# Feed-forward rows kept in PSUM, exponentials added before the row sum, a 128x9 reciprocal, and zero matmuls in PE's early gaps

## The chip, the core and the metric

The kernel runs on one core of one Trainium2 chip. The metric is device time in microseconds (us), from several timed runs, beside one execution that the hardware profiler recorded. PE is TensorE (matmuls), PEld its weight loads, DVE is VectorE, ACT is ScalarE, POOL is GpSimd, and SP issues the DMAs. PSUM is the accumulator memory that PE writes and that DVE and ACT read; SBUF is the working memory.

## The reference

Causal attention with a decaying bias over 8 batches of 8 heads (576 positions, head size 64), then a gated feed-forward on the joined heads:

```
cum    = cumsum(max(s, 0))
scores = q k^T / 8 + min(cum_k - cum_q, 0), causal
attn   = exp(scores - rowmax) / (sum + 1e-9)
x      = heads joined (attn v)                  # 576 x 512 per batch
h      = relu(x @ w_in)                         # 576 x 1024
conv   = sum over k of conv_w[k] * h shifted by k - 1 rows
out    = (h * sigmoid(conv)) @ w_out
```

## The kernel before

The 64 heads are worked as 32 pairs, four pairs to a batch. A pair p goes through these steps. Scores for the row maxima are made on PE into pairs of PSUM banks (`sh{p}.{i}`, lines 1089 to 1102) and reduced on DVE (lines 1124 and 1134); the maxima are transposed and come back by DMA as a shift row (`eq<-rt`, line 1179). Scores for the output are made transposed, keys on partitions (`sc{p}.{i}`, line 1211), and ACT turns them into exponentials in the tile `pt` (line 1233), in five blocks of keys t = 0 to 4 with 576, 448, 320, 192 and 64 query columns. The row sums (`sum{p}`, line 1289) are matmuls of `pt` with a one-hot matrix of 32 columns; the four quarters of the 576 queries, 144 columns each, go to four strips of the array, and the two heads run through the strips in opposite order. The product with v follows (`pv{p}`, line 1271). ACT copies the sums with a guard added (`gd{p}`, line 1308), DVE takes the reciprocal of the 128x144 tile (`inv{p}`, line 1313; only eight of its rows mean anything), SP stores it to DRAM (line 1318) and spreads it back to all partitions (line 1327, two DMAs), and DVE multiplies (`nm{p}`, line 1335). The high and low parts of the result become the tile `x` (lines 1350 and 1354).

The feed-forward works on halves of a batch. For each of eight blocks of 128 hidden columns a tile of 12 matmuls fills one PSUM bank (`h{b}.{hf}.{f}`, line 1386). ACT writes relu of it into the SBUF tile `ht` (line 1397), which frees the bank. Everything behind that is from SBUF: the scaled copy (line 1409), two taps on DVE (line 1422), one sigmoid for two blocks (line 1438), the product with `ht` (line 1444), and the split into high and low parts of `u` (lines 1451 and 1455). Output matmuls read `u` (`o{b}.{hf}.{m}.{fp}`, line 1483, 24 for a bank) and ACT or DVE evacuates them (line 1500).

Six PSUM banks (`ps`) serve all of this but `pv`, which has two of its own. The order on each engine isn't that of the program: `Sched.play` runs a list scheduler over all steps with assumed durations and the dates in the table `DUE`, and instructions are issued on each engine in the order that it finds; the semaphores then make each wait for its inputs. A bank is given to a step when the plan says that its last user is done. From pair 8 on, PE runs a pair's steps as one burst in a fixed order, which nothing else may interrupt:

```
ORDER = ("sh0", "sum", "pv", "sh1", "sc0", "sh2", "sc1", "sc2", "sh3", "sc3")
```

where `sum` and `pv` are of the pair before. The plan marks DVE and POOL steps that may disturb each other and doesn't let them overlap. It also models a slower PE after a rest (`REST`, `WARM`). `stay_awake` can fill PE's planned gaps until the time `AWAKE`; with `AWAKE = 0.0` it does nothing. In the first 160 us or so the weights are loaded as 64-bit words and taken apart on DVE, ACT and POOL (lines 863 to 952) beside the attention of the first pairs.

## Time and profile before

| | us |
|---|---|
| median of 3 runs (805.84 to 806.18) | 806.12 |
| the profiled execution | 809.6 |
| its span, first to last instruction | 807.9 |
| PE busy | 774.9 |
| DVE busy | 544.8 |
| ACT busy | 439.5 |
| POOL busy | 328.7 |

The profiled execution is 3.5 us longer than the median, and 1.7 us longer than its span. Busy times are modelled from the records; matmuls overlap, so a busy PE need not be PE at its peak.

### The profile page before, as it was taken

To read this page: it belongs to the slowest core of one execution; us is meant where nothing else is said; L and a number is where in the kernel's file an instruction comes from. 1 tells how busy PE (TensorE), PEld (TensorE's weight loads), DVE (VectorE), ACT (ScalarE), POOL (GpSimd) and SP (SyncE) were. 2 spreads that over 40 slices of the span, in tenths; PEclk is the share of its full clock that TensorE was granted. 3 is DMA by queue.
4 is the path that set the end of the run, shared out by engine and by line. 5 is a ranking of instruction groups with operands and counts; after the bars stand their busy time and mean duration, and the time that the engine had idled before them with its cause. 6 is when DMAs were issued, how large, how long until landed. Compare 5 with 4: busy or idle time off the path is not lost.

```text
span 807.9 us, 21422 instructions
## 1 busy us (share of the span) xinstructions
PE 774.9 (96%) x8557; PEld 690.7 (85%) x8557; DVE 544.8 (67%) x1310; ACT 439.5 (54%) x989; POOL 328.7 (41%) x508
## 2 busy tenths in 40 slices
PE   2899899999999999999999999999999999999998
PEld 1566566898999989998998989998898989998998
DVE  7789979747675867766566757667576576825532
ACT  5355446746455646546555646646554555744543
POOL 7122324344534455544435445553435454422122
PEclk9999989999999999999999999999999999999999
DMA  7654354221423232241414233241414221111001
GB/s 241 209 146 150 109 153 145 86 83 46 141 68 124 77 119 96 79 138 53 141 49 132 87 111 105 75 137 57 140 49 125 96 84 43 43 35 42 17 29 37
DMA packets 57369, 78.77 MB, mean 97 GB/s; under 512 B 6521, under 2 KB 39609, under 8 KB 57209
## 3 DMA queue, kind: packets, MB, share of 16 engines
q1 hardware_dynamic: 57269, 77.40, 30.2%
q8 instruction: 67, 1.10, 0.6%
q14 instruction: 33, 0.27, 0.1%
HBM read 63.94 MB, written 13.19 MB: 95 GB/s over the span
## 4 chain that ended last, share of the span: by engine, by line
PE 90%; DVE 4%; ACT 3%; DMA 1%; issue 1%; POOL 0%; SPq 0%; ACTq 0%; DVEq 0%; POOLq 0%
PE ps L1483 26%; PE ps L1386 25%; PE ps L1211 15%; PE pv L1271 11%; PE ps L1289 7%; PE ps L1089 4%; DVE ps L1134 2%; DMA ek<-bx 1%; PE ps L1101 1%; PE ps L1215 1%; ACT pt L1233 1%; PE ps L1095 1%; PE ps L1160 0%; ACT bx L784 0%; DVE ct L880 0%
## 5 line engine op out<-in xcount | busy, mean ns | idle before, releaser
L1483 PE MATMUL ps<-u,wo 128*128 128x288 f32 x1536 | 220.3, 299 | 0.7 <-ACT ob L1500 0.5
L1386 PE MATMUL ps<-x,wi 128*128 128x290 f32 x1536 | 217.5, 298 | 0.3 <-ACT pt L1233 0.2
L1422 DVE SCALAR_TENSOR_TENSOR ct<-ht,cw_sb,ct 128x288 f32<-128x288 f32 (+1 forms) x256 | 154.6, 617 | 84.7 <-ACT ct L1409 81.2
L1483 PEld LDWEIGHTS ps<-u,wo 128*128 128x128 f32 x1536 | 208.3, 188 | 3.6 <-ACT ob L1500 0.7
L1386 PEld LDWEIGHTS ps<-x,wi 128*128 128x128 f32 x1536 | 209.7, 190 | 1.4 <-ACT pt L1233 0.6
L1233 ACT ACTIVATE pt<-ps,bias_sb 128x288 f32<-128x288 f32 (+4 forms) x384 | 154.3, 478 | 88.7 <-PE ps L1211 88.1
L1455 POOL TENSOR_TENSOR u<-ct,u 128x576 fp32r<-128x576 f32 x64 | 94.2, 1477 | 234.2 <-ACT u L1451 201.0
L1134 DVE CUSTOM_DVE_ANT_0 ps<-ps,bb 128x288 f32<-128x288 f32 (+2 forms) x260 | 108.3, 454 | 60.0 <-PE ps L1089 30.6
L1211 PE MATMUL ps<-s 64*128 64x288 f32 (+4 forms) x1152 | 122.8, 309 | 5.7 <-DVE r L1134 4.2
L1066 POOL TENSOR_SCALAR_AFFINE_SELECT bb<-bb 128x256 f32<-128x256 f32 (+1 forms) x130 | 59.4, 466 | 129.5 <-DVE r L1134 102.3
L1211 PEld LDWEIGHTS ps<-s 64*128 64x128 f32 x1152 | 98.3, 190 | 15.7 <-DVE r L1134 10.0
L1025 POOL TENSOR_TENSOR s<-raw,s 128x1152 fp32r<-128x1152 f32 x31 | 83.2, 2684 | 48.1 <-DVE s L1021 36.8
L1271 PE MATMUL pv<-pt,v 128*32 128x448 f32 (+4 forms) x1536 | 96.6, 395 | 1.0 <-DVE rb L1335 1.0
L1397 ACT ACTIVATE ht<-ps 128x289 f32<-128x289 f32 x128 | 52.7, 411 | 80.0 <-PE ps L1386 79.3
L1271 PEld LDWEIGHTS pv<-pt,v 128*32 128x32 f32 x1536 | 60.0, 111 | 33.0 <-issue 26.2
L1246 POOL TENSOR_SCALAR_AFFINE_SELECT pt<-pt 128x128 f32<-128x128 f32 (+1 forms) x240 | 67.7, 302 | 22.0 <-ACT pt L1233 20.4
L1211 PE MATMUL ps<-eq,ek 64*128 64x288 f32 (+4 forms) x384 | 68.5, 323 | 0.0
L1409 ACT ACTIVATE ct<-ht,cw_sb 128x288 f32<-128x288 f32 x121 | 64.9, 536 | 5.4
L1089 PE MATMUL ps<-s 64*128 64x288 f32 (+4 forms) x384 | 61.9, 345 | 3.7 <-DVE r L1134 1.8
L1289 PE MATMUL ps<-pt,onehot 128*32 128x144 f32 (+4 forms) x1792 | 61.4, 273 | 0.2 <-ACT pt L1233 0.2
L1438 ACT ACTIVATE ct<-ct 128x576 f32<-128x576 f32 x64 | 43.5, 680 | 31.4 <-DVE ct L1422 30.6
L1289 PEld LDWEIGHTS ps<-pt,onehot 128*32 128x32 f32 x1792 | 54.8, 113 | 6.5 <-issue 1.1
(90 smaller groups left out, 671.0 us busy)
## 6 DMA issues: line engine op xcount, KB each, us to landing
raw<-qk SPq DMA_DIRECT2D x32, 576.0 KB
bb<-cum_d SPq DMA_DIRECT2D x26, 576.0 KB
v<-vp SPq DMA_DIRECT2D x32, 320.0 KB
rb<-ri_d SPq DMA_DIRECT2D x64, 144.0 KB
outT<-ob SPq DMA_DIRECT2D x64, 144.0 KB
ht<-w_out SPq DMA_DIRECT2D x16, 256.0 KB
w<-w_in SPq DMA_DIRECT2D x8, 512.0 KB
ri_d<-ri SPq DMA_DIRECT2D x32, 72.0 KB
```

The source lines that it names most:

```text
L1025: tt_on(e)(st[:, 0:2, :], R_t[raw.slot], st[:, 2:4, :].bitcast(F32), op=ALU.subtract)
L1089: nc.tensor.matmul(dst[j], l, S_t[sb.slot][r, 2, c0:c1], start=True, stop=not early)
L1134: nc.vector.tensor_tensor_reduce(out=src, in0=src, in1=in1, scale=1.0, scalar=acc if c0 else -3.0e38, op0=ALU.add, op1=ALU.max, accum_out=acc,
L1211: nc.tensor.matmul(dst[j], l, m, start=(k == 0), stop=(k == 3))
L1233: nc.scalar.activation(PT_t[pts[j].slot][0:jt, O_T[t] + c0 : O_T[t] + c1], bank(pb, o, o + c1 - c0)[0:jt], AF.Sigmoid, bias=bias_sb[0:jt, ...
L1246: nc.gpsimd.affine_select(out=reg, in_=reg, pattern=[[1, dg]], compare_op=ALU.is_ge, fill=0.0, base=0, channel_multiplier=-1,)
L1271: nc.tensor.matmul(pvt[gs, o0 : o0 + c1 - c0], vt[0:jt, t, gs], PT_t[pts[g // 2].slot][0:jt, O_T[t] + c0 : O_T[t] + c1], start=(t == 0), s ...
L1289: nc.tensor.matmul(bank(sb_, o0, o0 + b_ - a_)[32 * g : 32 * g + 32], onehot[:, j, :], src[:, a_ - c0 : b_ - c0], start=t == 0 and j == 0, ...
L1386: nc.tensor.matmul(bank(hb, 0, XW), l, r, start=(k == 0), stop=(k == len(seq) - 1))
L1422: nc.vector.scalar_tensor_tensor(cc[:, lo:hi], h_[:, sh + lo : sh + hi], cw_sb[:, 3 * f + k : 3 * f + k + 1], cc[:, lo:hi], op0=ALU.mult, ...
L1455: tt_on(e)(uu[:, 1], C_t[ct.slot], uu[:, 0].bitcast(F32), op=ALU.subtract)
L1483: nc.tensor.matmul(bank(pb, 0, HS), l, r, start=(fp == 0 and k == 0), stop=(fp == NF // 2 - 1 and k == len(seq) - 1),)
```

## The change

- **Row sums.** From pair 7 on (`D0`), DVE or POOL adds, for each head, key blocks 0 to 3 over the queries from 128 on into an accumulator that is a buffer of `ht` (`key_sum`: three additions, of 448, 320 and 192 columns). The row sum then has three blocks for a head: block 0 for the first 128 queries, the accumulator for the other 448, and block 4. It waits for the additions.
- **Reciprocal.** Two small DMAs gather the eight rows of sums into a 128x9 tile (`gather`), the reciprocal runs on that, and the store to DRAM has 4.6 KB in place of 72 KB. The spread reads the new layout.
- **Feed-forward.** relu is written back into the PSUM bank; the scaled copy, the taps and the product read the bank. The sigmoid and the product are done for each block of 288 columns, not for two at once. The bank is free after the product.
- **Zeros.** `stay_awake` is turned on until 112 us of the plan, with a zero tile: wherever the plan has no work for PE, a matmul of 256 columns of zeros into a free bank is put in, every 0.12 us of the plan.
- **Plan.** The slower PE after a rest is no longer modelled, and `DUE` has other values throughout.

The diff, without the table `DUE` and lines that only follow from these:

```diff
@@ -29,9 +29,10 @@
 NX = (5, 7)
 NBB = 2
 B1 = 6
+D0 = 7
 SCRATCH = 1024
-AWAKE = 0.0
-AWAKE_N, AWAKE_T = 256, 0.2
+AWAKE = 112.0
+AWAKE_N, AWAKE_T = 256, 0.12
...
-REST, WARM = 1.0, 3.4
...
+                        lane = [0]
+                        lanes[slot].append(lane)
+                        t.emit = lambda e, slot=slot, mode=mode, lane=lane: idle[4](
+                            slot, mode, lane[0]
+                        )
...
-                for b in got[0].alloc:
+                for j, b in enumerate(got[0].alloc):
                     b.slot = b.pool.fits(b.n)
                     b.pool.take(b.slot, b.n)
+                    if idle and b.pool is idle[5]:
+                        for lane in lanes.pop(b.slot, ()):
+                            lane[0] = j if got[0].mode == "r" else 0
...
-                    if now - rested > REST:
-                        cold = now + WARM
-                    if now < cold:
-                        dur = min(2 * dur, cold - now + (dur - (cold - now) / 2))
-                    rested = now + dur
...
+    still = const.tile([P, AWAKE_N], BF16, name="still")
...
-    ri_t = const.tile([P, RS], F32, name="ri")
+    RW = 2 * S // P
+    rc_t, ri_t = (const.tile([P, RW], F32, name=n) for n in ("rc", "ri"))
...
-    ri_d = dram.tile([P, RS], F32, name="ri_d")
+    ri_d = dram.tile([P, RW], F32, name="ri_d")
...
+    t_still = add("still", [("DVE", 0.2)], [], -300, lambda e: nc.vector.memset(still, 0.0))
...
+        dense = p >= D0
+        acc = [buf("ht"), buf("ht")] if dense else []
+        added = []
+        def partial(j):
+            return H_t[acc[j].slot].rearrange("p a c -> p (a c)")[:, 0 : S - P]
+        def key_sum(j, t):
+            def run(e):
+                a = partial(j)
+                src = PT_t[pts[j].slot]
+                o = P * (t - 1)
+                (nc.vector if e == "DVE" else nc.gpsimd).tensor_tensor(
+                    a[:, o:], src[:, P : S] if t == 1 else a[:, o:],
+                    src[:, O_T[t] : O_T[t] + W_T[t]], op=ALU.add,
+                )
+            return run
+        if dense:
+            for t in range(1, L):
+                for j in range(2):
+                    t_ad = add(
+                        f"ad{p}.{j}.{t}",
+                        [("DVE", c_tt(W_T[t]), True), ("POOL", c_pool(W_T[t]), True, 2.0)],
+                        [m for k, h, m in masks if h == j and (k == t or t == 1 and k == 0)]
+                        + ([added[-2]] if t > 1 else []),
+                        tq - 4, key_sum(j, t), alloc=[acc[j]] if t == 1 else [],
+                        uses=[pts[j]] + ([acc[j]] if t > 1 else []),
+                    )
+                    added.append(t_ad)
+        def sums(e):
+            if dense:
+                todo = [(0, 0), (1, 0), (0, 1), (1, 1), (L, 0), (L, 1)]
+            else:
+                todo = [(t, j) for t in range(NT) for j in range(2)]
+            for t, j in todo:
+                src = PT_t[pts[j].slot][:, O_T[t] : O_T[t] + W_T[t]]
+                c0 = P * t
+                c1 = P if dense and t == 0 else S
+                if dense and t == 1:
+                    src = partial(j)
+                for q in range(c0 // RS, 4):
+                    g = 3 - q if j else q
+                    a_, b_ = max(c0, q * RS), min(c1, (q + 1) * RS)
+                    if a_ >= b_:
+                        continue
+                    o0 = a_ - q * RS
+                    nc.tensor.matmul(
+                        bank(sb_, o0, o0 + b_ - a_)[32 * g : 32 * g + 32], onehot[:, j, :],
+                        src[:, a_ - c0 : b_ - c0], start=j == 0 and (t == 0 or dense and t == 1 and q > 0),
+                        stop=t == NT - 1, tile_position=(0, 32 * g), skip_group_check=True,
+                    )
...
+        t_sum = add(f"sum{p}", [("PE", 0.62 if dense else 1.5)], [t_ident] + [m for _, _, m in masks] + added,
+                    tq, sums, alloc=[sb_], uses=[*pts, *acc], mode="c32", burst=group(p + 1))
...
+        def gather(e):
+            for j in range(2):
+                nc.sync.dma_start(rc_t[j * D : (j + 1) * D], rs_t[j : 97 + j : 32])
+        t_rc = add(f"rc{p}", [("SP", 0.8)], [t_grd], tq, gather, uses=[ri], nbytes=4608)
         def inverse(e):
-            nc.vector.reciprocal(ri_t, rs_t)
-        t_inv = add(f"inv{p}", [("DVE", 1.06)], [t_grd], tq, inverse, uses=[ri])
+            nc.vector.reciprocal(ri_t, rc_t)
+        t_inv = add(f"inv{p}", [("DVE", 0.15)], [t_rc], tq, inverse, uses=[ri])
         def store_ri(e):
             nc.sync.dma_start(ri_d, ri_t)
-        t_ri = add(f"ri{p}", [("SP", 0.34)], [t_inv], tq, store_ri, uses=[ri], nbytes=73728)
+        t_ri = add(f"ri{p}", [("SP", 0.34)], [t_inv], tq, store_ri, uses=[ri], nbytes=4608)
...
-                    ri_d.tensor, ri_d.offset + (97 * RS if j else 0),
-                    [(0, D), (-32 * RS if j else 32 * RS, 4), (1, RS)],
+                    ri_d.tensor, ri_d.offset + (7 * RS if j else 0),
+                    [(0, D), (-RS if j else RS, 4), (1, RS)],
...
-        u, ht, ct = buf("u"), buf("ht"), buf("ct")
-        tg = h_tag(b, hf, 2 * fp)
-        taps, t_mm = [], None
+        u, ct = buf("u"), buf("ct")
+        products, t_mm = [], None
...
-            def relu(e, i=i, hb=hb):
+            def relu(e, hb=hb):
+                h = bank(hb, hf, hf + HS + 1)
+                nc.scalar.activation(h, h, AF.Relu)
+            t_relu = add(f"re{b}.{hf}.{f}", [("ACT", 0.41)], [t_mm], tg, relu, uses=[hb])
+            def center(e, i=i, f=f, hb=hb):
                 nc.scalar.activation(
-                    H_t[ht.slot][:, i, 0 : HS + 1], bank(hb, hf, hf + HS + 1), AF.Relu
+                    C_t[ct.slot][:, i, :], bank(hb, 2 * hf, 2 * hf + HS), AF.Copy,
+                    scale=cw_sb[:, 3 * f + 1 : 3 * f + 2],
                 )
-            t_relu = add(f"re{b}.{hf}.{f}", [("ACT", 0.41)], [t_mm], h_tag(b, hf, f), relu,
-                         uses=[hb, ht])
-            def center(e, i=i, f=f):
-                o = C_t[ct.slot][:, i, :]
-                src = H_t[ht.slot][:, i, hf : hf + HS]
-                w = cw_sb[:, 3 * f + 1 : 3 * f + 2]
-                if e == "ACT":
-                    nc.scalar.activation(o, src, AF.Copy, scale=w)
-                else:
-                    nc.vector.tensor_scalar(o, src, w, None, op0=ALU.mult)
-            t_c = add(f"ce{b}.{hf}.{f}", [("ACT", 0.53), ("DVE", 0.36, True, 2.0)],
-                      [t_relu, t_cw], h_tag(b, hf, f) + 0.1, center, uses=[ht, ct])
-            def tap(e, k, i=i, f=f):
-                h_ = H_t[ht.slot][:, i, :]
+            t_k = add(f"ce{b}.{hf}.{f}", [("ACT", 0.53)], [t_relu, t_cw], tg + 0.1, center,
+                      uses=[hb, ct])
+            def tap(e, k, i=i, f=f, hb=hb):
                 cc = C_t[ct.slot][:, i, :]
                 sh = hf + k - 1
                 lo = 1 if sh < 0 else 0
                 hi = HS - 1 if sh + HS > HS + 1 else HS
                 nc.vector.scalar_tensor_tensor(
-                    cc[:, lo:hi], h_[:, sh + lo : sh + hi],
+                    cc[:, lo:hi], bank(hb, hf + sh + lo, hf + sh + hi),
                     cw_sb[:, 3 * f + k : 3 * f + k + 1], cc[:, lo:hi],
                     op0=ALU.mult, op1=ALU.add,
                 )
-            t_k = t_c
             for k in (0, 2):
-                t_k = add(f"ta{b}.{hf}.{f}.{k}", [("DVE", 0.53, True)], [t_k],
-                          h_tag(b, hf, f) + 0.1, lambda e, k=k, tap=tap: tap(e, k), uses=[ht, ct])
-            taps.append(t_k)
+                t_k = add(f"ta{b}.{hf}.{f}.{k}", [("DVE", 0.53)], [t_k], tg + 0.1,
+                          lambda e, k=k, tap=tap: tap(e, k), uses=[hb, ct])
+            def gate(e, i=i):
+                cc = C_t[ct.slot][:, i, :]
+                nc.scalar.activation(cc, cc, AF.Sigmoid)
+            t_g = add(f"ga{b}.{hf}.{f}", [("ACT", c_act(HS))], [t_k], tg + 0.2, gate, uses=[ct])
+            def mul(e, i=i, hb=hb):
+                cc = C_t[ct.slot][:, i, :]
+                nc.vector.tensor_tensor(cc, cc, bank(hb, 2 * hf, 2 * hf + HS), op=ALU.mult)
+            products.append(add(f"mu{b}.{hf}.{f}", [("DVE", c_tt(HS))], [t_g], tg + 0.2, mul,
+                                uses=[hb, ct]))
...
-        def gate(e):
-            cc = C_t[ct.slot]
-            nc.scalar.activation(cc, cc, AF.Sigmoid)
-        t_g = add(f"ga{b}.{hf}.{fp}", [("ACT", c_act(2 * HS))], taps, tg, gate, uses=[ct])
-        def mul(e):
-            cc = C_t[ct.slot]
-            nc.vector.tensor_tensor(
-                cc, cc, H_t[ht.slot][:, :, hf : hf + HS], op=ALU.mult
-            )
-        t_m = add(f"mu{b}.{hf}.{fp}", [("DVE", c_tt(2 * HS), True)], [t_g], tg, mul, uses=[ct, ht])
...
-    def stay_awake(slot, mode):
-        r = slice(0, D if mode == "r" else P)
+    def stay_awake(slot, mode, lane):
+        r = slice(D * lane, D * lane + D) if mode == "r" else slice(0, P)
         nc.tensor.matmul(
-            ps_t[slot][:, 0:AWAKE_N], mask[r, 0:P], mask[r, 0:AWAKE_N], start=True, stop=True
+            ps_t[slot][:, 0:AWAKE_N], still[r, 0:P], still[r], start=True, stop=True
         )
     assert len(DUE) == len(sch.tasks)
     for t, due in zip(sch.tasks, DUE):
         t.tag = due / 16
     order = sch.play(
-        (AWAKE, t_ident, 0.005 + AWAKE_N * 0.42e-3, AWAKE_T, stay_awake, pool_ps)
+        (AWAKE, t_still, 0.005 + AWAKE_N * 0.42e-3, AWAKE_T, stay_awake, pool_ps)
```

## Rows read from the trace of the kernel before

**Rows 1.** The page: busy time, share and instructions of each engine

```profile
PE 774.9 (96%) x8557; PEld 690.7 (85%) x8557; DVE 544.8 (67%) x1310; ACT 439.5 (54%) x989; POOL 328.7 (41%) x508
```

**Rows 2.** Windows: length, busy (count) of PE, PEld, DVE, ACT, POOL; PEclk, DMA, GB/s

```profile
0.00:12.70 12.70, 0.00 (x0) 0.01 (x1) 10.62 (x19) 9.26 (x14) 11.13 (x28) 1.00 0.79 240
26.90:46.40 19.50, 19.40 (x153) 14.08 (x153) 12.23 (x34) 8.55 (x21) 4.72 (x3) 1.00 0.48 157
46.40:88.00 41.60, 40.81 (x522) 27.51 (x522) 39.11 (x85) 23.11 (x53) 9.37 (x5) 1.00 0.50 146
94.00:97.50 3.50, 3.50 (x28) 1.12 (x24) 3.15 (x12) 1.27 (x4) 1.86 (x3) 0.51 0.09 23
107.70:114.60 6.90, 6.90 (x87) 5.13 (x90) 4.74 (x16) 0.85 (x3) 2.04 (x4) 0.51 0.36 127
189.00:734.00 545.00, 539.74 (x6253) 498.20 (x6257) 365.68 (x902) 307.46 (x699) 246.29 (x422) 1.00 0.29 91
```

**Rows 3.** The chain that ended last: start, us, what, instructions

```profile
17.44 9.34 DMA ek<-bx
...
43.13 3.26 PE ps L1289 x44
...
181.72 6.44 PE ps L1386 x48
189.30 1.70 PE ps L1289 x40
191.05 2.70 PE pv L1271 x44
...
733.85 1.70 PE ps L1289 x40
```

**Rows 4.** Groups by line and shape: count, busy us, mean ns

```profile
L1422 DVE SCALAR_TENSOR_TENSOR ct<-ht,cw_sb,ct 128x288 f32<-128x288 f32 (+1 forms) x256 | 154.6, 617 | 84.7 <-ACT ct L1409 81.2
...
L1397 ACT ACTIVATE ht<-ps 128x289 f32<-128x289 f32 x128 | 52.7, 411 | 80.0 <-PE ps L1386 79.3
...
L1444 DVE TENSOR_TENSOR ct<-ct,ht 128x576 f32<-128x576 f32 x64 | 48.3, 756 | 15.2 <-ACT ct L1438 14.5
...
L1438 ACT ACTIVATE ct<-ct 128x576 f32<-128x576 f32 x64 | 43.5, 680 | 31.4 <-DVE ct L1422 30.6
...
L1313 DVE RECIPROCAL ri<-rs 128x144 f32<-128x144 f32 x32 | 33.6, 1049 | 12.8 <-ACT rs L1308 12.3
...
L1134 DVE CUSTOM_DVE_ANT_0 ps<-ps,bb 128x288 f32<-128x288 f32 x52 | 23.1, 470 | 25.0 <-PE ps L1089 22.4 <-ACT ht L1397 2.6
...
L876 ACT ACTIVATE ct<-ht 128x256 f32<-128x256 f32 x16 | 6.6, 436 | 0.3 <-DMA ht<-w_out 0.2
...
L952 DVE TENSOR_TENSOR wo<-ct,wo 128x256 fp32r<-128x256 f32 x10 | 4.2, 420 | 0.8 <-ACT wo L949 0.7
```

**Rows 5.** Waits of the weight loads: in total, times, longest us

```profile
PEld ps L1211 <- DVE r L1134: 10.0, 25, 0.6
```

**Rows 6.** Timeline of all engines, 88 to 92 us

```profile
88.28 2.70 POOL L1025 TENSOR_TENSOR s<-raw,s 128x1152 fp32r<-128x1152 f32 x1 [5.63 <-DVE s L1021]
...
88.40 2.86 DVE L880 SCALAR_TENSOR_TENSOR ct<-ht,ct 128x256 uint32<-128x256 uint32 x1
```

**Rows 7.** Timeline of all engines behind the last pair's row sum

```profile
738.82 0.33 SPq L1318 DMA_DIRECT2D ri_d<-ri  x1
...
740.54 1.24 SPq L1327 DMA_DIRECT2D rb<-ri_d  x2
...
744.30 0.76 DVE L1335 TENSOR_TENSOR rb<-pv,rb 128x576 f32<-128x576 f32 x1 [4.21 <-DMA rb<-ri_d]
...
747.18 0.75 DVE L1354 TENSOR_TENSOR x<-rb,x 128x580 fp32r<-128x580 f32 x1
...
748.22 2.04 PE L1386 MATMUL ps<-x,wi 128*128 128x290 f32 x14
```

More of the change, by code (lines that the diff above doesn't have):

```diff
@@ L388, in play @@
         now = awake = 0.0
-        rested, cold = -99.0, 0.0
+        lanes = collections.defaultdict(list)
         left = len(self.tasks)
@@ L461, in play @@
                         busy[e] = t
-                        if now - rested > REST:
-                            cold = now + WARM
-                        rested = now + idle[2]
-                        post(rested, "free", t)
+                        post(now + idle[2], "free", t)
                         awake = now + idle[3]
@@ L481, in play @@
                         dur += SW
-                    if now - rested > REST:
-                        cold = now + WARM
-                    if now < cold:
-                        dur = min(2 * dur, cold - now + (dur - (cold - now) / 2))
-                    rested = now + dur
                     mode = t.mode
@@ L1253, in pair @@
                                     A + 0.1 * i, sc_mask, uses=[pts[j]])
-                    masks.append((t, t_exp))
+                    masks.append((t, j, t_exp))
                     o += w
@@ L1277, in pv_mm @@
             return run
-        def sums(e):
-            for t in range(NT):
-                for j in range(2):
-                    src = PT_t[pts[j].slot][:, O_T[t] : O_T[t] + W_T[t]]
-                    c0 = P * t
-                    for q in range(c0 // RS, 4):
-                        g = 3 - q if j else q
-                        a_, b_ = max(c0, q * RS), (q + 1) * RS
-                        o0 = a_ - q * RS
-                        nc.tensor.matmul(
-                            bank(sb_, o0, o0 + b_ - a_)[32 * g : 32 * g + 32], onehot[:, j, :],
-                            src[:, a_ - c0 : b_ - c0], start=t == 0 and j == 0,
-                            stop=t == NT - 1, tile_position=(0, 32 * g),
-                            skip_group_check=True,
-                        )
@@ L1296, in pair @@
         ta = A1 + 1
         tq = ta - TQA
-        t_sum = add(f"sum{p}", [("PE", 1.5)], [t_ident] + [m for t, m in masks], tq, sums,
-                    alloc=[sb_], uses=pts, mode="c32", burst=group(p + 1))
-        t_pv = add(f"pv{p}", [("PE", 2.82)], [t_v] + [m for t, m in masks], tq + 0.1,
+        dense = p >= D0
[3 more added lines that the diff above has]
+            return H_t[acc[j].slot].rearrange("p a c -> p (a c)")[:, 0 : S - P]
@@ L1301, in pair @@
+        t_sum = add(f"sum{p}", [("PE", 0.62 if dense else 1.5)], [t_ident] + [m for _, _, m in masks] + added,
+                    tq, sums, alloc=[sb_], uses=[*pts, *acc], mode="c32", burst=group(p + 1))
+        t_pv = add(f"pv{p}", [("PE", 2.82)], [t_v] + [m for _, _, m in masks], tq + 0.1,
                    pv_mm(range(NT)), alloc=[pv], uses=[vb, *pts], mode="c32",
                    prev=None if p + 1 >= B0 else t_sum, burst=group(p + 1))
-        note(p + 1, "sum", t_sum, [t_v] + [m for t, m in masks])
+        note(p + 1, "sum", t_sum, [t_v] + [m for _, _, m in masks] + added)
@@ L1390, in moe_h @@
             xs = [x_bufs[b * HP + c][hf] for c in range(NC)]
+            tg = h_tag(b, hf, f)
             t_mm = add(f"h{b}.{hf}.{f}", [("PE", 1.61)],
                        [x_done[b * HP + c] for c in range(NC)] + [t_wi[f]],
[L1393 removed]
+                       tg, h_mm, alloc=[hb] + ([u, ct] if i == 0 else []),
                        uses=xs, prev=t_mm if i else None)
[L1396 removed]
+            def relu(e, hb=hb):
[3 more added lines that the diff above has]
+            def center(e, i=i, f=f, hb=hb):
                 nc.scalar.activation(
[L1398 to L1417 removed]
+                    C_t[ct.slot][:, i, :], bank(hb, 2 * hf, 2 * hf + HS), AF.Copy,
+                    scale=cw_sb[:, 3 * f + 1 : 3 * f + 2],
+                )
+            t_k = add(f"ce{b}.{hf}.{f}", [("ACT", 0.53)], [t_relu, t_cw], tg + 0.1, center,
+                      uses=[hb, ct])
+            def tap(e, k, i=i, f=f, hb=hb):
                 cc = C_t[ct.slot][:, i, :]
@@ L1458, in moe_h @@
                    [("DVE", c_cp(2 * HS), True, 1.0), ("ACT", c_act(2 * HS))],
-                   [t_m] + (list(t_wi.values()) if b == 0 else []), tg, u_hi,
+                   products + (list(t_wi.values()) if b == 0 else []), tg, u_hi,
                    uses=[ct, u])
```

3 lines of the change are left out of this document (removed), and 476 rows, old and new, of the table DUE.

## The prediction

> **What bounds the kernel now.** I read the page first: it puts TensorE (PE) at 96% of the span and VectorE (DVE) at 67% [rows 1]. The stretches come next, because an average hides stages: between the seventh pair's end and the last pair (189 to 734 us) PE is busy 539.74 of 545 us while DVE and ScalarE (ACT) have about a third or more of their time free [rows 2]. So in two thirds of the span a microsecond taken off PE's list is a microsecond of time. [...] Last I read the chain of waits and the waits themselves: what PE waits for is little, the largest entry for a bank that DVE has to free being 10.0 us in 25 waits [rows 5].
>
> All sums below are made against the profiled execution's own 809.6 us (span 807.9), which is 3.5 us above the median of the runs, 806.12; I take 3.5 off at the end.
>
> **Pre-added exponentials.** Pairs 7 to 31 replace five key blocks by three in the row sum: 12 matmuls instead of 28 for a pair, so 24 records instead of 56. Moving columns fall from 2 x 1600 to 2 x 640 (128 + 448 + 64 for a head), and in the fullest 32-column strip of the array from 800 to 352. From the start of a row sum to the start of the product behind it is 191.05 - 189.30 = 1.75 us [rows 3]. Scaled by records that becomes 0.75, by columns 0.70, by the fullest strip 0.77 us. The worst case is that the short blocks (128 and then 16 columns in one strip) hold up the other strips; then I allow 1.0 us. I take 0.75: 1.0 us saved, 25 times (first at 189.30, last at 733.85 [rows 3]) = **-25 us**, bounds -19 and -26.
>
> The additions themselves go to DVE or GpSimd: three for a head, over 448, 320 and 192 columns. A two-input DVE operation takes 420 ns for 256 columns and 756 for 576 [rows 4], so 1.05 ns a column and 0.15 us fixed: 0.62 + 0.49 + 0.35 = 1.46 us, 2.9 us for a pair, 73 us in all. What hides them is DVE's free time, 179 us of the 545 us stretch [rows 2]; they need only be done between a pair's exponentials and its row sum a burst later. The row sum now waits for them, and behind it, in PE's order, the whole burst. I take nothing. If the cover is gone, all 73 would show. One thing speaks for a collision: at 88.28 us a GpSimd subtraction of 2.70 us ran, and a DVE operation that began 0.12 us later, with two SBUF inputs, took 2.86 us where its like takes about 0.42 [rows 4, 6]. The additions have two SBUF inputs too.
>
> [...]
>
> **The 128x9 reciprocal.** DVE gives up 1.05 us and pays some 0.2 us (its shortest operations in the rows are the fixed 0.15 us above) [rows 4]: 0.85 us a pair, 27 us of DVE time, on PE's path nothing. Ahead of it come two small DMAs on SP's queue. The nearest rows are the DMAs of the last pair: the store was issued at 738.82, the spread that reads it at 740.54, and the product was released at 744.30 [rows 7]; a transfer therefore costs 1.7 to 3.8 us, and the gather about 3. The row sum reaches the normalized rows some 1 to 2 us later than before (3 - 0.85 - 1.0 from the shorter sum). The two issues take SP about 1.2 us, as the two of the spread do [rows 7], 32 times. Queued behind them on SP, and behind their wait for ACT's guarded copy, are the next loads, which are issued well ahead, and the shift row of the next scores, which is the one with a near date; it comes a whole burst later than a row sum. The only place where this is near the path is the last pair: x is ready just before the feed-forward matmuls at 748.22 [rows 7]. Output matmuls of the batch before still lie behind that point, so they can be drawn forward; I take 0, bounds 0 and +2.
>
> **Rows in PSUM.** Counts on PE don't change. On ACT the sigmoid is cut in two. One over 576 columns takes 680 ns and another function over 256 takes 436, so 288 columns take about 0.46 us [rows 4]: 64 x (2 x 0.46 - 0.68) = +15 us over the span, not on the path. On DVE the 256 taps now read PSUM: a custom operation of 288 columns with one PSUM input takes 470 ns against a mean of 617 for today's taps [rows 4], about -37 us; the product in two halves costs 64 x (2 x 0.47 - 0.76) = +12 us. DVE's total is then 545 + 73 - 27 - 37 + 12 = 566 us: still well below PE.
>
> What PE feels is the bank. Today ACT's one operation of 0.41 us frees it [rows 4]. Then it is held through relu, scaled copy, two taps, sigmoid and product: 0.41 + 0.46 + 2 x 0.47 + 0.46 + 0.47 = 2.7 us of work on two engines, some 3.1 us with the hand-overs, beside the 1.6 us in which it is filled (12 matmuls of 134 ns [rows 3]). A run of such tiles needs 4.7 / 1.6 = 3 banks of six, instead of 1.3, and an output tile two more. It fits, with little left for the burst that begins behind it. The bounds: 0, and 0.40 us (10.0 / 25, [rows 5]) for each of 128 tiles = +51 us. I take 0.2 us for each of some 25 bursts: **+5 us**, nearer the lower end, because the burst's first two steps need three banks and its third comes only 3.5 us later.
>
> **Zeros on PE.** A zero matmul has 256 columns; 290 take 134 ns [rows 3], so about 0.12 us each. PE does nothing for the first 12.7 us [rows 2] and has a few us free until 112 us, so the zeros take no time except where one is at work when the real one comes free: some 10 such cases, **+1 us**, bounds 0 and 4. What they may bring is the clock. [...] Together **-10 us**, bounds 0 and -15.
>
> [...]
>
> **Sum:** 809.6 - 25 - 10 + 5 + 1 = 780.6; less 3.5: **777 us**.
>
> **Rivals.** (1) *The banks decide.* If every feed-forward tile waits 0.40 us, 809.6 - 35 + 51 + 1 = 826.6, 823 at the median. For it: two engines with other work queued stand between a bank and its release. Against it: PE's present waits are small although DVE frees banks in every burst. It turns the sign from 36 / 128 = 0.28 us a tile.
> (2) *The start does not shrink*: zeros don't lift the clock, or DVE, busy 39.11 of 41.6 us after that [rows 2], is the bound as soon as PE is fast. Then 809.6 - 25 + 6 - 3.5 = 787.
> (3) *The additions are late.* They stall behind GpSimd as at 88 us and hold up the burst's start by half a microsecond 25 times: 777 + 12 = 789. [...]
> (4) *It all comes off*: sum at its lower bound, clock at 13 us, no bank waits: 809.6 - 26 - 13 - 3.5 = 767.
>
> **How the numbers follow.** Forecast 0.46, rival 1 0.10, rival 2 0.17, rival 3 0.13, rival 4 0.14. The forecast's own range is 770 to 784. With rivals 2 to 4 the range is **762 to 797**, which leaves out rival 1 and the far ends of the others. Within 0.2% (1.6 us, about what a measurement of this kernel can tell) of the old time lies only a narrow piece of rival 1 or of a mixture: 0.02; slower 0.08, faster **0.90**.
>
> **What would show it.** The group of the row sum should fall from 56 to 24 records and to about 0.75 us for pairs 7 and up. The first row sum should take about 1.8 us and begin near 36 us, with no stretch at 0.5 before 115 us. Waits of PE on DVE's product or on ACT for a bank should stay under 15 us in all. DVE should be busy about 566 us. I am wrong if PE's share of the span falls by more than two points in the middle stretch, if DVE passes 90% there, or if the first row sum still takes over 3 us.

## The result, and the profile after

The changed kernel takes 781.05 us (median; 780.34 to 784.16), the kernel before 806.15 in the same comparison: a ratio of 0.970 [0.967, 0.972], 25 us less. The forecast was 777, its range 762 to 797. The profiled execution took 780.34 us, 29.3 less than that of before (809.6). A second profiled execution of the same kernel, from the comparison with the experiments, took 784.72; below it shows how much the start of this kernel varies.

The page of the changed kernel, engines (as in [rows 1]):

```profile
PE 759.4 (98%) x7975; PEld 680.1 (87%) x7975; DVE 529.8 (68%) x1460; ACT 453.7 (58%) x1065; POOL 379.9 (49%) x561
```

Its windows, three stretches of [rows 2], then from the first short row sum to the last, and a short one within that:

```profile
26.90:46.40 19.50, 19.46 (x248) 13.94 (x250) 17.10 (x45) 10.52 (x25) 4.80 (x3) 1.00 0.60 188
...
94.00:97.50 3.50, 3.50 (x38) 2.81 (x38) 1.94 (x5) 3.15 (x9) 0.88 (x1) 1.00 0.75 223
107.70:114.60 6.90, 6.90 (x83) 5.80 (x83) 4.83 (x16) 5.15 (x15) 4.60 (x5) 1.00 0.52 162
173.30:694.50 521.20, 508.41 (x5388) 464.93 (x5386) 356.68 (x1009) 317.73 (x746) 293.09 (x470) 0.99 0.30 92
...
238.00:241.40 3.40, 3.40 (x46) 2.53 (x48) 1.02 (x5) 0.96 (x2) 1.41 (x1) 0.50 0.29 92
```

In this execution the start has no stretch at the lower level behind 26.9 us any more (26.9 to 46.4 us holds 248 matmuls in place of 153, the two short ones read 1.00 in place of 0.51). The lower level is a granted clock of 0.50 to 0.51: in the window of 30 to 42.5 us, which run 1 shows, the second execution read 0.50 and held 78 matmuls, this one 1.00 and 184. The kernel before held 79 there, so by its rate it was at the lower level too, though its granted clock reads 1.00:

```profile
30.00:42.50 12.50, 12.42 (x79) 8.84 (x80) 7.80 (x20) 7.76 (x19) 3.13 (x2) 1.00 0.43 143
```

But the long stretch, where before PE stood idle for 5.3 of 545 us, now has 12.8 idle in 521.2, and two short falls of the clock (the last line shows one; the other, at 613.5 us, is as long). So behind the start something new makes PE wait.

The chain that ended last (its shares by line, then pieces):

```profile
by line: PE ps L1454 25.6%; PE ps L1543 24.3%; PE ps L1235 13.0%; PE pv L1295 11.4%; PE ps L1113 4.2%; PE ps L1354 4.0%; issue 2.9%; DVE ps L1158 1.4%; DVE ht L1318 1.3%; DMA ek<-bx 1.2%; PE ps L1125 1.1%; PE ps L1239 1.0%; ACT pt L1257 0.8
...
37.64 1.77 PE ps L1354 x41
...
173.34 0.73 PE ps L1354 x16
...
174.13 2.70 PE pv L1295 x44
```

From the start of a short row sum to the product behind it is 174.13 - 173.34 = 0.79 us, where it was 1.75 [rows 3]. And VectorE's additions (`DVE ht L1318`) are on the chain with 1.3% of it, 10 us: they were to be hidden.

How the profiled executions divide, cut at the starts of the eighth and of the last pair's row sum (matmul records of the sums):

```
                                start   middle   tail    end
before                          189.2    544.6   74.1   807.9
changed                         173.3    521.2   84.0   778.5
changed, second execution       179.4    519.6   84.0   782.9
changed, without zeros          183.4    519.5   84.0   786.9
changed, without zeros, second  181.3    517.8   84.0   783.2
before, with zeros, same order  186.3    544.6   74.1   804.9
changed, full row sums          174.3    532.5   85.0   791.8
changed, one addition per head  176.1    510.2   83.7   770.0
changed, 128x144 reciprocal     179.9    529.2   84.1   793.2
```

The tail is 9.9 us longer because the new order leaves more matmuls for it, which the middle has less of: 264 instead of 192 of `h`, and 312 instead of 294 of the output. Windows of the tail, output matmuls alone (length, busy (count) of PE and PEld, PEclk, DMA, GB/s), first of the kernel before, then of the changed one:

```profile
733.78:807.90 74.12, 41.21 (x294) 39.83 (x294) 1.00 0.10 32
```

```profile
694.50:778.50 84.00, 43.21 (x312) 41.93 (x312) 0.99 0.09 29
```

72 of 134 ns (6.44 us for 48, [rows 3]) are 9.6 us, and 18 of some 133 ns are 2.4: 12.0 us in all. At equal work the middle is 23.4 - 12.0 = 11.4 us shorter, the tail 2.1, and the start 10 to 16.

### The profile page after: what moved, and what is told of

Its sections match the earlier page's. It is cut to its first block, busy times and chain, and to the rows that moved or that the text cites. A ratio compares the mean times of both kernels' runs of the same rounds, so it can differ in the third digit from the quotient of the medians.

```text
span 778.5 us, 20786 instructions
## 1 busy us (share of the span) xinstructions
PE 759.4 (98%) x7975; PEld 680.1 (87%) x7975; DVE 529.8 (68%) x1460; ACT 453.7 (58%) x1065; POOL 379.9 (49%) x561
## 4 chain that ended last, share of the span: by engine, by line
PE 86%; DVE 5%; issue 3%; ACT 3%; POOL 1%; DMA 1%; SPq 0%; DVEq 0%; ACTq 0%; POOLq 0%
PE ps L1454 26%; PE ps L1543 24%; PE ps L1235 13%; PE pv L1295 11%; PE ps L1113 4%; PE ps L1354 4%; DVE ps L1158 1%; DVE ht L1318 1%; DMA ek<-bx 1%; PE ps L1125 1%; PE ps L1239 1%; ACT pt L1257 1%; PE ps L1590 1%; PE ps L1184 1%; DVE r L1158 1%
## 5 line engine op out<-in xcount | busy, mean ns | idle before, releaser
L1454 PE MATMUL ps<-x,wi 128*128 128x290 f32 x1536 | 221.1, 300 | 4.5 <-DVE ct L1503 4.1
L1485 DVE SCALAR_TENSOR_TENSOR ct<-ps,cw_sb,ct 128x288 f32<-128x288 f32 (+1 forms) x256 | 131.1, 514 | 76.2 <-ACT ct L1472 73.3
L1235 PE MATMUL ps<-s 64*128 64x288 f32 (+4 forms) x1152 | 118.5, 303 | 5.6 <-DVE r L1158 4.8
L1049 POOL TENSOR_TENSOR s<-raw,s 128x1152 fp32r<-128x1152 f32 x31 | 84.5, 2726 | 51.6 <-DVE s L1045 32.0
L1090 POOL TENSOR_SCALAR_AFFINE_SELECT bb<-bb 128x256 f32<-128x256 f32 (+1 forms) x130 | 55.8, 437 | 82.1 <-DVE ri L1381 39.8
L1467 ACT ACTIVATE ps<-ps 128x289 f32<-128x289 f32 x128 | 50.8, 397 | 61.9 <-PE ps L1454 58.0
L1270 POOL TENSOR_SCALAR_AFFINE_SELECT pt<-pt 128x128 f32<-128x128 f32 (+1 forms) x240 | 73.3, 327 | 19.5 <-ACT pt L1257 18.6
L1497 ACT ACTIVATE ct<-ct 128x288 f32<-128x288 f32 x128 | 56.4, 440 | 40.9 <-DVE ct L1485 40.3
L1503 DVE TENSOR_TENSOR ct<-ct,ps 128x288 f32<-128x288 f32 x128 | 57.4, 449 | 28.2 <-ACT ct L1497 27.5
L1472 ACT ACTIVATE ct<-ps,cw_sb 128x288 f32<-128x288 f32 x128 | 64.0, 500 | 5.1
L1318 DVE TENSOR_TENSOR ht<-ht,pt 128x192 f32<-128x192 f32 (+1 forms) x80 | 60.0, 784 | 7.9 <-POOL pt L1270 7.0
L1113 PE MATMUL ps<-s 64*128 64x288 f32 (+4 forms) x384 | 57.3, 330 | 3.4 <-ACT ct L1497 2.0
```

What stands on the lines that cost most here:

```text
L1049: tt_on(e)(st[:, 0:2, :], R_t[raw.slot], st[:, 2:4, :].bitcast(F32), op=ALU.subtract)
L1113: nc.tensor.matmul(dst[j], l, S_t[sb.slot][r, 2, c0:c1], start=True, stop=not early)
L1235: nc.tensor.matmul(dst[j], l, m, start=(k == 0), stop=(k == 3))
L1270: nc.gpsimd.affine_select(out=reg, in_=reg, pattern=[[1, dg]], compare_op=ALU.is_ge, fill=0.0, base=0, channel_multiplier=-1,)
L1318: (nc.vector if e == "DVE" else nc.gpsimd).tensor_tensor(a[:, o:], src[:, P : S] if t == 1 else a[:, o:], src[:, O_T[t] : O_T[t] + W_T[t]] ...
L1454: nc.tensor.matmul(bank(hb, 0, XW), l, r, start=(k == 0), stop=(k == len(seq) - 1))
```

## The experiments

Ratios are to the kernel before, run on the same chip; 0.01 is 8.1 us. Two kernels that did not run in the same comparison are compared by their ratios. The kernels marked "same order" issue on each engine what the changed kernel (or the one before) issues there, in its order, except for the edit.

**1. No zeros** (changed kernel, same order; run twice).

```diff
     def stay_awake(slot, mode, lane):
+        return
```

> The changed kernel with every other instruction in its place, but without the 154 zero matmuls. Theory (the zeros bring the clock, and PE sets the pace from 27 us on): the first row sum again takes about 3.3 us, a stretch at the lower clock comes back before 115 us, and the time is 781 + 10 = 791 us (787 to 795). Rival (DVE or the DMAs set the start, the clock is beside the point): 781 to 783 us, whatever the first row sum takes.

Measured: 785.08 us, ratio 0.973 [0.969, 0.978].

> The changed kernel without its zero matmuls again, now beside the changed kernel itself. The first look left 3 us by the medians and 8 us by the profiled executions. If the zeros are worth what the lower clock costs at the start: 8 to 10 us above the changed kernel; if later work of other engines takes most of it up: 2 to 5 us.

Measured: 786.2 us, 0.973 [0.970, 0.976], beside 781.59, 0.968 [0.964, 0.972] of the changed kernel in the same comparison. The zeros (218 matmuls in the trace, not the 154 of the expectation) are worth some 3 to 5 us, not 10: 3 by the ratios of the first run and the changed kernel, 4 to 5 in this comparison, where the single runs of the two kernels, 784.94 to 788.13 and 779.14 to 785.95, just overlap.

Two things make it less. The first was missed by forecast and expectation alike: without zeros the first row sum does not take 3.3 us again. Timeline of PE without zeros (start, length, what, [idle before]):

```profile
42.16 1.59 PE L1354 MATMUL ps<-pt,onehot 128*32 128x144 f32 x48 [0.29 <-ACT rt L1191]
```

These 48 of its 56 records take 1.59 us, where 44 took 3.26 in the kernel before [rows 3]: in the new order PE is at the higher level by then without help. What returns without zeros are lower stretches behind it (granted clock 0.50 from 72.3 to 79.0 and from 92.9 to 96.2 us in this execution).

The second is that the zeros don't always keep the clock up. Timeline of PE in the changed kernel, first the profiled execution of the first comparison, then the second one, then that of run 3 below, which has the same start:

```profile
13.81 2.67 PE L1590 MATMUL ps<-still 128*128 128x256 bf16 x23
...
26.81 0.60 PE L1125 MATMUL ps<-ek,eb 64*128 64x288 f32 x2 [0.59 <-DMA ek<-bx]
```

```profile
27.03 0.60 PE L1125 MATMUL ps<-ek,eb 64*128 64x288 f32 x2 [0.82 <-DMA ek<-bx]
```

```profile
27.61 0.62 PE L1125 MATMUL ps<-ek,eb 64*128 64x288 f32 x2 [0.86 <-DMA ek<-bx]
```

Windows of 30 to 42.5 us, of the three in this order:

```profile
30.00:42.50 12.50, 12.50 (x184) 9.24 (x183) 11.38 (x28) 7.61 (x19) 2.77 (x1) 1.00 0.54 180
```

```profile
30.00:42.50 12.50, 12.50 (x78) 8.93 (x78) 6.59 (x16) 7.02 (x18) 2.49 (x1) 0.50 0.42 139
```

```profile
30.00:42.50 12.50, 12.48 (x178) 9.17 (x181) 11.26 (x30) 7.54 (x19) 2.77 (x1) 1.00 0.57 185
```

Up to this transfer the executions ran alike, at the higher level: 23 zero matmuls of 256 columns in 2.67 us are 116 ns each, as 290 columns in 134 ns [rows 3]. In the first PE stood 0.59 us for it and stayed there; in the second it stood 0.82 us and then ran at the lower level for the whole window, with 78 matmuls in the time of 184; in the third it stood 0.86 us and stayed at the higher level. So with the zeros the clock is up by 13.8 us, and at this transfer it can be lost again; the length of the wait alone doesn't decide it, and what does stays open. Of the nine profiled executions that have this start with zeros, six fell to the lower level there (waits of 0.82 to 1.83 us) and three did not (0.59, 0.86 and 0.86). Where it fell, the first row sum began at 40.5 to 43.0 us, otherwise at 37.6 to 38.5; without zeros it began at 42.2 and 41.8.

**2. Zeros in the kernel before**, first with the plan made anew around them, then with the order of before kept.

```diff
-AWAKE = 0.0
-AWAKE_N, AWAKE_T = 256, 0.2
+AWAKE = 112.0
+AWAKE_N, AWAKE_T = 256, 0.12
```

> The kernel before with the zero matmuls alone, put into PE's planned gaps until 112 us. Theory: the clock is up before 15 us, the first row sum takes 1.8 us and comes 6 us or more earlier, and the time falls by about 10 us, to 796 (792 to 800). Rival (the start is bound by DVE and DMA): 804 to 807 us. If the zeros helped only because the plan was made anew for them: between the two.

Measured: 819.51 us, 1.016 [1.011, 1.020]: slower. The run doesn't tell what zeros do, since with them the planner put the work into another order: from the start to the eighth row sum it needed 196.2 us (189.2 before), with the same middle and tail.

> The kernel before with its order of the work unchanged on every engine, and the zero products (174 of them) put beside it into banks that are free and hold no row yet, up to the sixth pair. Theory (zeros are worth what taking them out of the changed kernel cost, 4.6 us, whatever kernel they stand in): 801 to 803 against 806 to 809, and the first row of sums before 40 us in place of 43.1. First theory, the forecast's: minus 10, because all lower stretches before 115 us go. Rival: what the start gains is given back at a later wait of the hand-written order, so nothing: within 2 us of the kernel before. Rival: zeros stand in front of real products, so slower by some us, as in the run in which the order was made anew.

Measured: 805.6 us, 0.9975 [0.995, 0.9999]: 2 us, nearest in time to the rival in which the start's gain is lost again. But there was no gain to lose at first: its first row sum began at 43.6 us and took 3.3, as in the kernel before. Its windows:

```profile
16.00:18.00 2.00, 0.00 (x0) 0.00 (x0) 0.29 (x2) 0.00 (x0) 0.42 (x2) 1.00 0.48 59
...
20.00:22.00 2.00, 2.00 (x14) 1.22 (x14) 1.43 (x6) 0.00 (x0) 0.10 (x1) 0.50 1.30 494
```

PE found nothing to do from 16 to 18 us (zeros stand only where the plan saw a hole) and was at the lower level behind it (0.50 from 20 to 22 us), and again when the first row sum began (0.50 from 40 to 44 us).

**3. Full row sums** (same order): PE adds all five blocks itself, and no addition is issued.

```diff
             def run(e):
+                return
                 a = partial(j)
...
         def sums(e):
+            dense = False
```

(`dense` is set aside inside the sums alone.)

> The changed kernel in the same order, but the row sums of pairs 7 to 31 read the five blocks of exponentials again and the 150 additions are not issued. Theory (PE's list sets the time and the additions cost it nothing): the step from row sum to product goes from 0.79 back to 1.75 us, 25 x 0.96 = +24, so 805 us (801 to 808). Rival (the additions are late and hold up the bursts by half a microsecond): taking them away gives back about 12 us, so 793 us (788 to 797).

Measured: 796.09 us, 0.987 [0.982, 0.991]: 14 us over the changed kernel, where 24 is what the shorter sums save. Some 10 us are paid for the additions, so the theory fell, and the time lies in the rival's range.

**4. One addition for a head** (same order): the short sums as they are, the second and third addition not issued, so the sums lack two of the key blocks.

```diff
             def run(e):
+                if t > 1:
+                    return
                 a = partial(j)
```

> The changed kernel in the same order, without the second and third addition of each head, so that the sums lack key blocks 2 and 3; 100 of 150 operations are left out and PE's work stays. Theory (the additions lie in free time of DVE and GpSimd): 780 to 782 us, within 2 us of the changed kernel. Rival (they are late, or stall DVE behind GpSimd where PE waits for DVE): 6 to 12 us less, 769 to 775 us.

Measured: 771.97 us, 0.957 [0.953, 0.961]: 9 to 10 us faster than the changed kernel, though a third of the additions is still there. Windows of the stretch between the eighth and the last row sum, of run 3 and of run 4:

```profile
174.30:706.80 532.50, 526.01 (x6158) 484.22 (x6156) 288.53 (x909) 316.15 (x746) 240.35 (x426) 1.00 0.30 90
```

```profile
176.10:686.30 510.20, 504.28 (x5387) 462.03 (x5385) 303.13 (x932) 317.78 (x746) 271.48 (x451) 1.00 0.31 94
```

PE is idle 6.5 and 5.9 us there against 12.8 in the changed kernel, and the clock no longer falls. Where the time comes back can be read by laying the matmul records of run 4 beside those of the changed kernel, one by one: behind 170 us the changed kernel loses 11.0 us to it, some 5 of them at the first matmuls of `h` tiles, 2.9 at scores, 3.2 in the two short stretches at the lower clock, and next to nothing at the start of the short sums. The sums themselves don't wait; the additions hold up what stands behind them on VectorE. The changed kernel's groups and timelines of VectorE and GpSimd show how:

```profile
L1485 DVE SCALAR_TENSOR_TENSOR ct<-ps,cw_sb,ct 128x288 f32<-128x288 f32 (+1 forms) x256 | 131.1, 514 | 76.2 <-ACT ct L1472 73.3
...
L1318 DVE TENSOR_TENSOR ht<-ht,pt 128x192 f32<-128x192 f32 (+1 forms) x80 | 60.0, 784 | 7.9 <-POOL pt L1270 7.0 <-ACT pt L1257 0.3
...
L1503 DVE TENSOR_TENSOR ct<-ct,ps 128x288 f32<-128x288 f32 x128 | 57.4, 449 | 28.2 <-ACT ct L1497 27.5
```

```profile
231.15 4.62 DVE L1318 TENSOR_TENSOR ht<-ht,pt 128x192 f32<-128x192 f32 x1
235.70 0.44 DVE L1503 TENSOR_TENSOR ct<-ct,ps 128x288 f32<-128x288 f32 x1
```

```profile
231.24 2.67 POOL L1049 TENSOR_TENSOR s<-raw,s 128x1152 fp32r<-128x1152 f32 x1
233.88 1.32 POOL L1423 TENSOR_TENSOR x<-rb,x 128x580 fp32r<-128x580 f32 x1
```

An addition of 192 columns, shortest 0.34 us, takes 4.62 while two subtractions of GpSimd run in a row beside it, to 235.20 us. Behind it on VectorE stand product and taps, behind these a bank, and PE stops from 235.70 to 237.63 us; the fall of the clock at 238 us follows. Behind 150 us, 9 of the 105 additions on VectorE take over 2 us, and those over 1.5 times the median of their size exceed it by 27 us together.

Only five of the nine are followed by a stop of PE, and the trace shows which. Between the eighth and the last row sum PE has five stops of over half a microsecond. Timeline of PE:

```profile
237.63 0.41 PE L1113 MATMUL ps<-s 64*128 64x288 f32 x2 [1.95 <-ACT ct L1497]
...
327.61 0.40 PE L1113 MATMUL ps<-s 64*128 64x288 f32 x2 [0.80 <-DVE ct L1503]
...
346.11 0.67 PE L1454 MATMUL ps<-x,wi 128*128 128x290 f32 x3 [1.55 <-DVE ct L1503]
...
522.61 0.67 PE L1454 MATMUL ps<-x,wi 128*128 128x290 f32 x3 [0.63 <-DVE ct L1503]
...
612.24 0.53 PE L1454 MATMUL ps<-x,wi 128*128 128x290 f32 x2 [1.92 <-DVE ct L1503]
```

Each comes 6 to 7 us behind the start of a long addition, the first behind the one at 231.15 us, the others behind these:

```profile
321.37 2.84 DVE L1318 TENSOR_TENSOR ht<-ht,pt 128x192 f32<-128x192 f32 x1
...
339.53 2.98 DVE L1318 TENSOR_TENSOR ht<-ht,pt 128x320 f32<-128x320 f32 x1
...
515.84 3.16 DVE L1318 TENSOR_TENSOR ht<-ht,pt 128x320 f32<-128x320 f32 x1
...
605.41 3.65 DVE L1318 TENSOR_TENSOR ht<-ht,pt 128x192 f32<-128x192 f32 x1
```

All five run beside GpSimd's subtraction `s` (L1049), which takes 2.65 to 2.80 us there. The stops are 6.9 us in all, and the two lower stretches behind the first and the last of them cost 3.2: 10 of the 11.0 us. The second execution and both runs without zeros have the same five stops; runs 3 and 4 have none of this length. The 256 taps, which now have one input in PSUM, don't stand at all: 514 ns on the mean where it was 617 [rows 4], and 521 at most.

**5. All additions on GpSimd, or all on VectorE** (same order; the second run has `nc.vector` in this place). The changed kernel issues 45 of 150 on GpSimd.

```diff
-                (nc.vector if e == "DVE" else nc.gpsimd).tensor_tensor(
+                nc.gpsimd.tensor_tensor(
```

> The changed kernel in its own order, with all 150 additions issued on GpSimd in place of 45 there and 105 on VectorE. VectorE loses 81 us of work and GpSimd gains about 88 (1.15 us for a first addition, 0.75 for a later one), so it is 60% busy in place of 49%. Theory (the 10 us that the additions give back are their standing on VectorE behind GpSimd's operations, 24 us over their median in all): faster by 4 to 8 us, 773 to 777, no addition over 1.5 us. Rival (what counts is that the three additions of a head are late at all): GpSimd's own queue of masks, u and s makes them later still, slower by 5 to 15 us, and the products wait for masks of GpSimd.

Measured: 805.49 us, 0.996 [0.993, 1.000]: 21 to 23 us slower than the changed kernel by the ratios. My theory fell, and the rival's 5 to 15 was too small. The group of the other two-input operation that is left on VectorE, and one of its kind in the timeline:

```profile
L1423 DVE TENSOR_TENSOR x<-rb,x 128x580 fp32r<-128x580 f32 x18 | 64.3, 3570 | 13.1 <-ACT x L1419 13.1
```

```profile
187.53 5.97 DVE L1423 TENSOR_TENSOR x<-rb,x 128x580 fp32r<-128x580 f32 x1 [1.66 <-ACT x L1419]
```

The standing only changes place: `x` takes 3.57 us in place of 0.96, and PE waits for it (10.0 us in 4 waits at `h`).

> The changed kernel in its own order, with all 150 additions issued on VectorE. GpSimd loses 44 us, VectorE gains 24 to 30 and has 45 more operations with two inputs in SBUF that can stand behind GpSimd's. Theory (standing behind GpSimd is what the additions cost): slower by 2 to 6 us, 783 to 787. Rival (the turns between the engines cost, and a head's additions in one queue are sooner done): the same or faster by 1 to 3 us. Beside the run with all of them on GpSimd this tells which engine's lateness counts.

Measured: 780.81 us, 0.967 [0.963, 0.971]: no change that can be measured, so the first theory's 2 to 6 us are not there. VectorE has 45 more additions, and 12 of its 150 take over 2 us in place of 9 of 105, yet PE has five stops of over half a microsecond again, at the same places. So the number of long ones doesn't set the cost; it depends on what stands behind them, as the five stops show. No run moved a single one of them.

**6. GpSimd's subtractions in pieces** (same order): `s` in four, `u` in two, so that VectorE might come in between.

```diff
-            tt_on(e)(uu[:, 1], C_t[ct.slot], uu[:, 0].bitcast(F32), op=ALU.subtract)
+            for a in range(2):
+                tt_on(e)(uu[:, 1, a], C_t[ct.slot][:, a], uu[:, 0, a].bitcast(F32), op=ALU.subtract)
```

> The changed kernel in the same order, with GpSimd's two long subtractions cut: the 1152-column one into four, the 576-column one into two. Theory from the runs with fewer additions (nine additions on DVE took 2.4 to 4.6 us because they stood behind such a subtraction, and what DVE then frees late, PE waits for): no DVE operation stands longer than about 1.5 us, and 4 to 8 us of the 10 that the additions cost come back, 773 to 777 us. Rival (the additions cost by their own 75 us of DVE and GpSimd time, not by standing): 780 to 783 us, or a little more for GpSimd's extra instructions.

Measured: 786.65 us, 0.973 [0.970, 0.977]: slower by 4 to 5 us beside the changed kernel of the same comparison. Its timeline, VectorE and then GpSimd:

```profile
236.61 5.02 DVE L1324 TENSOR_TENSOR ht<-ht,pt 128x192 f32<-128x192 f32 x1
```

```profile
236.69 3.09 POOL L1054 TENSOR_TENSOR s<-raw,s 128x288 fp32r<-128x288 f32 x4
239.74 1.32 POOL L1429 TENSOR_TENSOR x<-rb,x 128x580 fp32r<-128x580 f32 x1
```

The pieces follow each other without a hole, and VectorE's addition did not end between them: it now takes 5.02 us, through four pieces and the next operation. PE's stop behind it is 2.31 us in place of 1.95. The theory fell.

**7. Rows in SBUF** (same order): relu into an SBUF tile, scaled copy, taps and product from there.

```diff
-                nc.scalar.activation(h, h, AF.Relu)
+                nc.scalar.activation(row(hf, hf + HS + 1), bank(hb, hf, hf + HS + 1), AF.Relu)
...
-                    cc[:, lo:hi], bank(hb, hf + sh + lo, hf + sh + hi),
+                    cc[:, lo:hi], row(hf + sh + lo, hf + sh + hi),
```

> The changed kernel in the same order, but relu writes the feed-forward row into SBUF again and everything behind reads it there, so that PE's wait for a bank ends with relu. Theory of the forecast (the held banks cost PE about 5 us, the taps from PSUM save DVE time that is free anyway): 776 to 779 us. Rival (reading PSUM keeps the taps from standing behind GpSimd, and this is worth more than the banks): 784 us or more, with taps at about 0.6 us in place of 0.51.

Measured: 825.5 us, 1.020 [1.015, 1.025]: 42 us over the changed kernel of the same comparison. Its groups (profiled execution 833.5 us, at the long end of its runs):

```profile
L1488 DVE SCALAR_TENSOR_TENSOR ct<-gt,cw_sb,ct 128x288 f32<-128x288 f32 (+1 forms) x256 | 169.5, 670 | 65.5 <-ACT ct L1475 62.9
L1506 DVE TENSOR_TENSOR ct<-ct,gt 128x288 f32<-128x288 f32 x128 | 78.9, 618 | 28.8 <-ACT ct L1500 26.5
```

Taps of 670 ns instead of 514 and products of 618 instead of 449: 38 + 22 us more on VectorE, nearly all of it standing (the longest tap 4.56 us; the median tap takes 518 ns, in the changed kernel 516). The order was made for rows in PSUM, so 42 us is what PSUM is worth in this order, not what the change gained by it.

**8. The 128x144 reciprocal** in the changed kernel (same order), without the gather; store and spread take the 128x144 tile as before.

```diff
-            nc.vector.reciprocal(ri_t, rc_t)
+            nc.vector.reciprocal(ri_t, rs_t)
```

> The changed kernel in its own order, but with the reciprocal taken over 128x144 as before and the gather's two transfers left out. Theory (the forecast's 0: the chain behind the sums is hidden behind some 20 us of a pair's other work): within 2 us of the changed kernel, though VectorE has 32 reciprocals of about 0.95 us in place of 0.21, 24 us more. Rival (VectorE's time counts now, as it did for the additions): slower by 3 to 6 us. Other rival: the gather's landing of about 2 us is on the path of the normalizing products, so faster by 1 to 3 us.

Measured: 795.28 us, 0.985 [0.982, 0.989]: 13 us slower than the changed kernel. My 0 fell, and the rival's 3 to 6 was too small. Waits of the weight loads, first of the changed kernel, then of this one (total, times, longest):

```profile
PEld ps L1235 <- DVE r L1158: 11.1, 28, 0.6
```

```profile
PEld ps L1235 <- DVE r L1158: 21.0, 51, 0.9
```

Timelines of VectorE, the changed kernel, this one, and the kernel before:

```profile
314.41 0.52 DVE L1158 CUSTOM_DVE_ANT_0 ps<-ps,bb,r 128x288 f32<-128x288 f32 x1
...
314.85 0.21 DVE L1381 RECIPROCAL ri<-rc 128x9 f32<-128x9 f32 x1
314.98 0.21 DVE L1158 CUSTOM_DVE_ANT_0 ps<-ps,bb 128x64 f32<-128x64 f32 x1
```

```profile
321.88 0.52 DVE L1158 CUSTOM_DVE_ANT_0 ps<-ps,bb,r 128x288 f32<-128x288 f32 x1
...
322.32 1.05 DVE L1380 RECIPROCAL ri<-rs 128x144 f32<-128x144 f32 x1
323.29 0.21 DVE L1158 CUSTOM_DVE_ANT_0 ps<-ps,bb 128x64 f32<-128x64 f32 x1
```

```profile
346.28 1.05 DVE L1313 RECIPROCAL ri<-rs 128x144 f32<-128x144 f32 x1 [1.21 <-ACT rs L1308]
349.02 0.53 DVE L1134 CUSTOM_DVE_ANT_0 ps<-ps,bb,r 128x288 f32<-128x288 f32 x1 [1.69 <-PE ps L1089]
```

In the kernel before, the reciprocal lies in a hole of VectorE, with 1.21 us free ahead and 1.69 behind; there its width costs nothing. With the gather it comes some 3 us later, and that is between two row maxima whose banks the scores need at once: there 0.84 us of width are 0.4 us of PE, in 23 more waits, 10 of the 13 us. So gather and narrowing belong together, and the narrowing alone can't be undone. What the pair is worth against the wide reciprocal in its old place no run shows.

No kernel that computes the whole was measurably faster than the changed one.

## Why the prediction was right

The total came out 4 us from the forecast, but only in part for the forecast's reasons. Two steps were too favourable, the additions by 10 to 12 us and the clock by 5 to 7; what made up for them was a term taken too high (banks, +5) and a gain that was not in the forecast (the order at the start). That they cancel is luck.

- **Row sums, -25: right.** 24 records, 0.79 us where 0.75 was forecast: (1.75 - 0.79) x 25 = 24 us.
- **"I take nothing" for the additions: failed.** They cost 10 to 12 us (run 4: 9 to 10 by the ratios, with a third of them still there; run 3 beside the changed kernel: the middle shrinks by 11.3 where 24 sums save 23). This is rival 3 in its cause, standing behind GpSimd, and by chance in its price, 12, but not in its place: it said half a microsecond at each burst's start. The runs show five operations of 2.8 to 4.6 us, which delay product and taps, and with them `h` and the scores. The forecast compared the additions with VectorE's free time as a sum; the cover has to be free at the moment at which something stands behind them. The collision that the forecast read at 88 us is what came: all nine additions of over 2 us run beside GpSimd's subtraction `s`, the longest 4.62 us, while no tap, with one input in PSUM, takes over 0.52.
- **The clock from zeros, -10: too large.** No run shows the 10; the runs show 3 to 5 us in its place (run 1), and the zeros' own price, +1, is in that. The profiled execution of the first comparison came near the forecast (no stretch at 0.5 before 115 us, the first sum takes 1.77 us and begins at 37.6), but in six of nine the clock falls at the wait for pair 1's rows. And in the new order the first row sum is at the higher level without zeros too (run 1), so the shorter time of that sum is not theirs. In the order of before the zeros bring 2 us. Rival 2, the start that does not shrink, fell: it is 10 to 16 us shorter, though the zeros are less than half of that. Zeros alone came up to the higher level: 22 of them fall into the 4.5 us from 1.1 us on, 64 into the 6.8 us from 5.9 us on, and at 13.8 us they run at 116 ns, with no other matmul before them.
- **Rows in PSUM, +5: too large; their waits come with the additions.** PE's waits on the product and on ACT's operations for a bank are 4.1 + 2.0 + 0.8 us, under the 15 that were named:

```profile
PE ps L1454 <- DVE ct L1503: 4.1, 3, 1.9
PE ps L1113 <- ACT ct L1497: 2.0, 1, 2.0
...
PE ps L1113 <- DVE ct L1503: 0.8, 1, 0.8
```

  These are the five stops of run 4, so they belong to the additions; in runs 3 and 4, which hold the banks as long, PE has no such wait. What the rows' place saves can't be separated from the order made for it: at equal work, the run with full sums and no additions has a middle of 532.5 where before's would be 544.6 - 12.0 = 532.6, and a tail of 85.0 where it would be 86.1, so rows in PSUM, reciprocal and new order together give about 1 us behind the start. Rival 1, banks that decide, is excluded: it wanted over 0.28 us for each of 128 tiles, 36 us (34 by the terms of its own sum, 0.27 a tile).
- **The reciprocal, 0: not contradicted, but not measured by itself.** Run 8 shows only that the wide one costs 13 us at the new place.
- **What was not in the forecast: the new order at the start.** Without zeros the start is still 6 to 8 us shorter than before (183.4 and 181.3 against 189.2). The forecast took the order as given and changed only durations in it.

Summed by what was measured: sums -24, additions +10 to 12, zeros -3 to -5, the order at the start -6 to -8, the rest -1: 22 to 28 less, beside 25 by the medians and 29 by the profiled executions. The first three are from runs; the order's share is what is left at the start, no run has it alone. VectorE is busy 529.8 us and not 566, in part since 45 additions went to GpSimd (24 us at VectorE's medians).

## What to carry to other kernels

Work put on an engine with much free time is free only if nothing urgent stands behind it in that engine's queue at that moment: read the timeline around the place where it will be issued, not the engine's share (VectorE is 68% busy, and the additions cost 10 to 12 us). Here 0.34 us of VectorE work with two SBUF inputs became 4.62 beside 4.0 us of GpSimd's, so I would price such an operation with GpSimd's whole run beside it; of the 256 taps with an input in PSUM none took over 0.52 us. When a plan is made anew with a change, what a run without one part of it in the same order shows is that part's worth in that order (13 us for the reciprocal, 42 for the rows), which need not be what it brought.

## What the hardware showed that I had not expected

- A VectorE addition of 0.35 us stood 4.62 us beside two operations of GpSimd, 5.02 beside five shorter ones that had no hole between them, and a subtraction of 0.75 us 5.97 beside a longer run.
- The clock: at one and the same wait of PE it fell in six executions and stayed up in three, and the wait's length alone doesn't tell which (0.82 us and it fell, 0.86 and it stayed). In the second profiled execution of the changed kernel it fell for over 12 us and the first row sum came 5.4 us later than in the first. That is most of the difference between the two at the eighth row sum (173.3 and 179.4).
